# Top-k attention with an ELU feed-forward: the start-up order, the queue of the first queries, and the buffers of the weight decoding

## The chip, the cores and the metric

The kernel runs on one core of a Trainium2 chip. A core has five engines that run side by side[...]: TensorE (PE, matrix products; its weight loads are shown apart as PEld), VectorE (DVE), ScalarE (ACT), GpSimd (POOL) and SyncE (SP), which here only issues DMAs. The metric is the device time of one execution in microseconds (us), median of three runs.

## The reference

```python
def _attn_ref(q, k, v):            # each (8, 8, 576, 64) float32
    scores = 1/sqrt(64) * q @ k.transpose(0, 1, 3, 2)
    kth = the 32nd largest of each row of 576 scores
    scores = where(scores >= kth, scores, -1e9)
    attn = exp(scores - max); attn = attn / (sum(attn) + 1e-9)
    return attn @ v

def _moe_ref(x, w_in, w_out):      # x (4608, 512), w_in (512, 2048), w_out (2048, 512)
    h = x @ w_in
    g = where(h > 0, h, exp(min(h, 0)) - 1)
    return g @ w_out
```

The attention's output (batch, head, position, feature) is reordered to (batch x position, head x feature) and is the input x of the feed-forward part. The weights arrive as float64 and are decoded to float32 on the core. The output is 4608 x 512 float32.

## The kernel before, in words

**Attention steps.** The work is cut into steps of 128 query rows for one pair of heads: `scores` (L298 on PE, evacuated by ACT at L306) makes a 128 x 576 score tile for each of two heads. VectorE finds the 32 largest of each row by four MAX8 and three MATCH_REPLACE8 per head (L317, L321, L327 in the first eight steps; L339, L344, L351 later). `mask` makes two small POOL operations (L364, L366) and two ACT passes, a steep PReLU and an Exp with a row sum (L367, L368). `normalise` adds a small constant on POOL (L377), takes the reciprocal on VectorE (L379) and scales the tile on POOL (L381). `turn` transposes the tile on PE (L400) and ACT copies it out (L401); `attend` multiplies with v (L426), and `finish` copies the result into xT (L453). Scores are made two steps ahead.

**Start-up.** `load_qk(b, hp)` loads keys and queries of a head pair by three DMAs each (L221, L225), `load_v` the values by four (L236, L243); all are issued on SP, whose queue is in order. `transpose_qk` turns keys and queries on PE (L256, L268), and ACT copies them out (L261, L274).

**Feed-forward.** When a block of 1 to 3 tiles of 128 tokens is complete, `hidden(f)` makes 128 hidden features of it: four accumulating matmuls (L484, eight in the profile), a ReLU of the negative into a tile `n` (L496), a ReLU into gT (L497), an Exp (L498); a later VectorE operation (L465, from `close_gates`) joins n and gT. `project` (L507) multiplies with w_out. The pieces are handed out by `feed`, a written plan of costs and due times; a piece is held back until `decoded[0]` says that the weights that it needs are decoded.

**Weight decoding.** 32 pieces (16 of w_in, 16 of w_out) of 128 x 512 weights. `load_weight` brings 512 KB (4 KB for each partition) by one SP DMA (L150) into a buffer of the pool `raw`. `convert_first` runs three ACT passes (L167, L168, L169) and a POOL clamp (L170, which needs L167). `convert_last` runs two VectorE operations (L177, which needs L170; L180) and a POOL addition (L184) that writes the weights and lets the buffer go. `decode_piece(i)` asks for the load of piece i+2, converts piece i by `convert_first`, and ends piece i-1 by `convert_last`; it is called from `hook`, between VectorE's selection passes.

**What sets the order.** Up to step 8 (`tight`) a scheduler places the instructions of each engine; from step 8 on PE, ACT, VectorE and POOL keep the written order (`manual_schedule`). On each engine instructions then run in that order.

Of the kernel before, what the change touches and what calls it, by code (L numbers as in the profile page):

```python
# [8 lines left out]
AF = mybir.ActivationFunctionType  # L9
ALU = mybir.AluOpType  # L10
FP32 = mybir.dt.float32
U32 = mybir.dt.uint32
# [68 lines left out]
def kernel(  # L81
# [27 lines left out]
    def pool(name, bufs, **kw):  # L109
        return ctx.enter_context(tc.tile_pool(name=name, bufs=bufs, **kw))  # L110
# [5 lines left out]
    wkpool = pool("wk", 1)  # L116
    etpool = pool("et", 2)
    small = pool("small", 4)
    xtpool = pool("xt", 2)
    opool = pool("o", 1)  # L120
    ps_sc = pool("ps_sc", 1, space=PSUM)
    ps_t = pool("ps_t", 2, space=PSUM)
# [3 lines left out]
    raws = ExitStack()  # L126
    early = raws.enter_context(tc.tile_pool(name="early", bufs=1))
    earlyf = raws.enter_context(tc.tile_pool(name="earlyf", bufs=4))
    rawpool = raws.enter_context(tc.tile_pool(name="raw", bufs=3))

    ident = const.tile([P, P], FP32, tag="ident", name="ident")
    make_identity(nc, ident[:])
# [13 lines left out]
        return moe_w_out[f * P : (f + 1) * P, :], w_out[:, f, :]  # L146

    def load_weight(i):
        t = rawpool.tile([P, 4 * WN], U32, tag="raw", name="raw")
        nc.sync.dma_start(t[:, 0 : 2 * WN], weight(i)[0])  # L150
        raw[i] = t

    def parts(t):
        words = t[:, 0 : 2 * WN].rearrange("p (n w) -> p n w", w=2)
        return words[:, :, 0], words[:, :, 1], t[:, 2 * WN : 3 * WN], t[:, 3 * WN :]

    def convert_first(i):

        lo, hi, e, m = parts(raw[i])
        ef, mf = e.bitcast(FP32), m.bitcast(FP32)
        nc.scalar.activation(ef, hi.bitcast(FP32), AF.Abs, scale=2.0**-48)  # L167
        nc.scalar.activation(mf, lo, AF.Copy, scale=2.0**-29, bias=2.0**23)  # L168
        nc.scalar.activation(m.bitcast(I32), mf, AF.Copy, bias=-(2.0**23))  # L169
        nc.gpsimd.tensor_scalar(  # L170
            ef, ef, (2.0 - 2.0**-3 - 2.0**-23) * 2.0**-32, 2.0**-63, ALU.min, ALU.max
        )

    def convert_last(i):
        t, dst = raw.pop(i), weight(i)[1]
        lo, hi, e, m = parts(t)
        nc.vector.tensor_scalar(  # L177
            e, e, 0x0FFFFFFF, 3, ALU.bitwise_and, ALU.logical_shift_left
        )
        nc.vector.scalar_tensor_tensor(  # L180
            out=e, in0=hi, scalar=0x80000000, in1=e,
            op0=ALU.bitwise_and, op1=ALU.bitwise_or,
        )
        nc.gpsimd.tensor_tensor(  # L184
            dst.bitcast(I32), e.bitcast(I32), m.bitcast(I32), ALU.add
        )

    decode = []
# [2 lines left out]
    def hook():  # L191

        if not decode:
            return
        decode.pop(0)()
        if not decode:
            raws.close()
            late["f"] = ctx.enter_context(tc.tile_pool(name="f", bufs=5))
            late["g"] = ctx.enter_context(tc.tile_pool(name="g", bufs=2))
            late["x"] = ctx.enter_context(tc.tile_pool(name="x", bufs=2))  # L200

    def decode_piece(i):
        if i < 2 * NF:
            if i + 2 < 2 * NF:
                load_weight(i + 2)
            convert_first(i)
        if i > 0:
            convert_last(i - 1)
            decoded[0] = i

    loaded, kqT, vT = {}, {}, {}

    def load_qk(b, hp):

        for name, src in (("k", k), ("q", q)):
            n = J + 1 if name == "k" else J
            t = ldpool.tile([P, n, 2, D], FP32, tag=name + "in", name=name + "in")
            if name == "k":
                last = t
            for hh in range(2):  # L220
                nc.sync.dma_start(  # L221
                    t[:, 0:J, hh, :],
                    src[b, 2 * hp + hh, 0:JP, :].rearrange("(p j) d -> p j d", j=J),
                )
            nc.sync.dma_start(  # L225
                last[0:R, J, :, :] if name == "k" else last[R:P, J, :, :],
                src[b, 2 * hp : 2 * hp + 2, JP:S, :].rearrange("h p d -> p h d"),
            )
            loaded[b, hp, name] = t

    def load_v(b, hp):

        t = kvpool.tile([P, 2 * J + 2, D], FP32, tag="vT", name="vT")
        for hh in range(2):
            h = 2 * hp + hh
            nc.sync.dma_start(  # L236
                t[:, hh * J : (hh + 1) * J, :],
                v[b, h, 0:JP, :].rearrange("(p j) d -> p j d", j=J),
            )
            mine = slice(hh * R, (hh + 1) * R)  # L240
            other = slice((1 - hh) * R, (2 - hh) * R)
            nc.gpsimd.memset(t[other, 2 * J + hh, :], 0.0)
            nc.sync.dma_start(t[mine, 2 * J + hh, :], v[b, h, JP:S, :])  # L243
        vT[b, hp] = t
# [32 lines left out]
    def start_qk(b, hp):  # L277
        turning.append(transpose_qk(b, hp))

    def turn_qk(whole=False):  # L280
        while turning:
            if next(turning[0], turning) is turning:
                turning.pop(0)
            elif not whole:
                return
# [3 lines left out]
    def scores(u):  # L289

        u.sc = scpool.tile([P, 2, S], FP32, tag="sc", name="sc")
        q0 = QUERIES + u.t.qt * P
        for half in range(2):
            for h, i, rows in u.heads:
                kq = kqT[u.t.b, h // 2]
                part = slice(i * D, (i + 1) * D)
                k0 = (KEYS if i == 0 else 0) + half * HS
                nc.tensor.matmul(  # L298
                    wide[rows, 2 * i + half, 0:HS],
                    kq[part, q0 : q0 + u.t.ql],  # L300
                    kq[part, k0 : k0 + HS],
                    start=True,
                    stop=True,
                )
        for i in range(2):
            nc.scalar.activation(  # L306
                u.sc[:, i, :].rearrange("p (a s) -> p a s", a=2),
                wide[:, 2 * i : 2 * i + 2, 0:HS], AF.Copy, scale=scale,
            )
# [136 lines left out]

    def finish(blk, parts, at, cols, src):
        if blk.xT is None:
            if blk.slots == 1 and late:
                blk.xT = late["x"].tile([P, NC, P], FP32, tag="xT", name="xT")  # L450
            else:
                blk.xT = xtpool.tile([P, NC, T], FP32, tag="xT", name="xT")
        nc.scalar.copy(blk.xT[:, at, cols], src)  # L453
        blk.left -= parts
        if blk.left == 0:
            ffn.extend(ffn_pieces(blk))
# [150 lines left out]
            fed["sum"] += cost  # L607
            piece()

    load_qk(0, 0)  # L610
    for i in range(2):
        load_weight(i)
    load_qk(0, 1)
    load_v(0, 0)
    start_qk(0, 0)
    turn_qk(True)
    scores(steps[0])
    load_qk(0, 2)
    start_qk(0, 1)
    turn_qk(True)  # L620
    scores(steps[1])
    load_qk(0, 3)
    for hp in range(1, NHP):
        load_v(0, hp)
    decode += [lambda i=i: decode_piece(i) for i in range(2 * NF + 1)]
    at(0, start_qk, 0, 2)
    at(1, start_qk, 0, 3)

# [5 lines left out]
    for n in range(NS + 3):  # L634
        for fn, args in todo.pop(n, []):
            fn(*args)
        ahead, cur, prev, done = step(n + 2), step(n), step(n - 1), step(n - 2)
        if n < tight:
            turn_qk(True)
            scores(ahead)  # L640
            for i in range(2):
                passes = select_row(cur, i)
                next(passes)
                if i == 0:
                    while closing:
                        attend(closing.pop(0))
                elif prev:
                    normalise(prev)
                    turn(prev, main)
                    turn(prev, rest)  # L650
                    turn(prev, other)
                feed(n, 0.25)
                next(passes)
                mask(cur, i)
                feed(n, 0.25)
            continue
        if n == tight:
            E = mybir.EngineType
            ctx.enter_context(
                tc.manual_schedule(engines={E.PE, E.Activation, E.DVE, E.Pool})  # L660
            )
        passes = select(cur) if cur else iter(range(4))
        if ahead:
            scores(ahead)
        while closing:
            attend(closing.pop(0))
        next(passes)
        feed(n, 0.25)
        if prev:
            mask(prev, 0)  # L670
        turn_qk()
        next(passes)
        feed(n, 0.25)
        if done:
            turn(done, main)
            turn(done, rest)
        if prev:
            mask(prev, 1)
        next(passes)
        feed(n, 0.25)  # L680
        if done:
            turn(done, other)
        next(passes)
        if prev:
            normalise(prev)
        feed(n, 0.25)
        turn_qk(True)
# [36 lines left out]
```

## Time and profile before

| what | value |
|---|---|
| median of 3 runs | 1712.81 us (1712.72 to 1713.59) |
| the profiled execution, its own time | 1713.55 us |
| its span, first to last instruction | 1711.8 us |
| PE busy | 1593.9 us (93%), 8560 matmuls |
| DVE busy | 1551.1 us (91%) |
| ACT busy | 1180.3 us (69%) |
| POOL busy | 432.7 us (25%) |
| mean granted TensorE clock | 0.973 |

Times in the profile are microseconds from the span's start; a line such as `L177` is a line of the kernel before. The page splits the span into 40 slices of 42.8 us and gives the busy share of each engine in tenths. A group of instructions is shown with its busy time, the mean time of one in nanoseconds, and the idle time of its engine just before it, with the instruction that ended this idle time. The chain is followed back from the last instruction, at each step to what released it. Busy is not the same as at full speed: an instruction that waits inside the engine for a shared resource counts as busy.

### The profile page before, as it was taken

To read this page: it belongs to the slowest core of one execution; us is meant where nothing else is said; L and a number is where in the kernel's file an instruction comes from. 1 tells how busy PE (TensorE), PEld (TensorE's weight loads), DVE (VectorE), ACT (ScalarE), POOL (GpSimd) and SP (SyncE) were. 2 spreads that over 40 slices of the span, in tenths; PEclk is the share of its full clock that TensorE was granted. 3 is DMA by queue.
4 is the path that set the end of the run, shared out by engine and by line. 5 is a ranking of instruction groups with operands and counts; after the bars stand their busy time and mean duration, and the time that the engine had idled before them with its cause. 6 is when DMAs were issued, how large, how long until landed. Compare 5 with 4: busy or idle time off the path is not lost.

```text
span 1711.8 us, 26507 instructions
## 1 busy us (share of the span) xinstructions
PE 1593.9 (93%) x8560; PEld 1029.6 (60%) x8560; DVE 1551.1 (91%) x3392; ACT 1180.3 (69%) x2813; POOL 432.7 (25%) x1142
## 2 busy tenths in 40 slices
PE   4558999999999999999999999999999999999999
PEld 3345676667575666655557575755557575755565
DVE  7899999999999999999999999999989999998600
ACT  5886786778686776768658585867758686767531
POOL 3664222222222222222222222222222212222100
PEclk8569999999999999999999999999999999999999
DMA  6531021001100111001100111001100000000000
GB/s 168 171 126 54 15 48 35 7 7 43 48 7 7 29 35 41 1 15 41 43 18 1 34 35 35 7 13 40 32 26 7 21 21 28 7 7 7 7 13 13
DMA packets 101130, 56.24 MB, mean 33 GB/s; under 512 B 84096, under 2 KB 92288, under 8 KB 100992
## 3 DMA queue, kind: packets, MB, share of 16 engines
q1 hardware_dynamic: 100992, 54.55, 11.5%
q8 instruction: 68, 1.11, 0.3%
q14 instruction: 70, 0.57, 0.1%
HBM read 45.09 MB, written 9.44 MB: 32 GB/s over the span
## 4 chain that ended last, share of the span: by engine, by line
PE 64%; DVE 23%; ACT 8%; issue 3%; POOL 1%; DMA 1%; SPq 0%; ACTq 0%; POOLq 0%
PE ops L507 25%; PE hps L484 19%; DVE wk L344 8%; PE avps L426 7%; DVE m L351 7%; PE scps L298 6%; PE eps L400 4%; DVE m L339 2%; DVE gT L465 2%; ACT sc L367 2%; ACT sc L368 2%; DVE wk L321 1%; DVE m L327 1%; ACT et L401 1%; ACT n L498 1%
## 5 line engine op out<-in xcount | busy, mean ns | idle before, releaser
L484 PE MATMUL hps<-xT,w_in 128*128 128x256 f32 (+2 forms) x2432 | 555.7, 377 | 24.8 <-ACT gT L497 16.9
L351 DVE MAX8 m<-wk 128x8 f32<-128x576 f32 x816 | 574.9, 745 | 0.0
L507 PE MATMUL ops<-w_out,gT 128*128 128x512 f32 x1152 | 522.6, 598 | 0.0
L484 PEld LDWEIGHTS hps<-xT,w_in 128*128 128x128 f32 x2432 | 410.1, 194 | 126.0 <-ACT gT L497 23.8
L344 DVE MATCH_REPLACE8 wk<-m,wk 128x576 f32<-128x576 f32 x544 | 399.5, 741 | 0.0
L507 PEld LDWEIGHTS ops<-w_out,gT 128*128 128x128 f32 x1152 | 208.6, 190 | 232.8 <-issue 197.5
L381 POOL TENSOR_SCALAR sc<-sc,rec 128x576 f32<-128x576 f32 x288 | 218.8, 769 | 254.7 <-DVE rec L379 234.0
L367 ACT ACTIVATE sc<-sc,neg 128x576 f32<-128x576 f32 x288 | 226.6, 787 | 55.9 <-POOL neg L364 55.6
L377 POOL TENSOR_SCALAR dene<-den 128x2 f32<-128x2 f32 x144 | 34.4, 239 | 879.5 <-ACT sc L368 878.9
L368 ACT ACTIVATE sc<-sc,gap 128x576 f32<-128x576 f32 x288 | 223.2, 775 | 26.3 <-ACT sc L367 1.5
L306 ACT ACTIVATE sc<-scps 128x576 f32<-128x576 f32 x288 | 173.0, 660 | 80.5 <-PE scps L298 80.4
L401 ACT COPY et<-eps 128x512 f32<-128x512 f32 x288 | 167.2, 581 | 74.3 <-PE eps L400 74.2
L426 PE MATMUL avps<-et,vT 128*64 128x256 f32 (+2 forms) x2080 | 190.4, 324 | 14.3 <-ACT et L401 13.7
L400 PE MATMUL eps<-ident,sc 128*128 128x128 f32 x1152 | 177.8, 280 | 24.7 <-POOL sc L381 24.6
L400 PEld LDWEIGHTS eps<-ident,sc 128*128 128x128 f32 x1152 | 145.2, 145 | 92.2 <-issue 48.4
L344 DVE MATCH_REPLACE8 wk<-m,sc 128x576 f32<-128x576 f32 x272 | 199.7, 741 | 0.0
L298 PE MATMUL scps<-kqT 64*128 64x288 f32 (+1 forms) x1280 | 186.5, 440 | 11.1 <-ACT et L401 6.1
L339 DVE MAX8 m<-sc 128x8 f32<-128x576 f32 x272 | 191.2, 744 | 0.0
L496 ACT ACTIVATE n<-hps 128x256 f32<-128x256 f32 (+2 forms) x304 | 112.4, 370 | 91.9 <-PE hps L484 89.0
L465 DVE SCALAR_TENSOR_TENSOR gT<-n,gT 128x256 f32<-128x256 f32 (+2 forms) x304 | 128.9, 430 | 49.6 <-ACT n L498 49.6
L426 PEld LDWEIGHTS avps<-et,vT 128*64 128x64 f32 x2080 | 120.6, 140 | 87.8 <-issue 28.7
L298 PEld LDWEIGHTS scps<-kqT 64*128 64x128 f32 (+1 forms) x1280 | 100.2, 182 | 76.6 <-issue 22.2
(43 smaller groups left out, 1066.1 us busy)
## 6 DMA issues: line engine op xcount, KB each, us to landing
kin<-in_k_dram SPq DMA_DIRECT2D x64, 128.0 KB, 2.8
qin<-in_q_dram SPq DMA_DIRECT2D x64, 128.0 KB, 2.8
raw<-in_moe_w_in_dram SPq DMA_DIRECT2D x16, 512.0 KB, 4.1
vT<-in_v_dram SPq DMA_DIRECT2D x64, 128.0 KB, 2.2
raw<-in_moe_w_out_dram SPq DMA_DIRECT2D x16, 512.0 KB, 3.2
out_dram<-osb SPq DMA_DIRECT2D x32, 256.0 KB, 2.2
kin<-in_k_dram SPq DMA_DIRECT2D x32, 32.0 KB, 2.5
kin<-in_q_dram SPq DMA_DIRECT2D x32, 32.0 KB, 2.3
```

Of the source, the lines that this page charges most:

```text
L298: nc.tensor.matmul(wide[rows, 2 * i + half, 0:HS], kq[part, q0 : q0 + u.t.ql], kq[part, k0 : k0 + HS], start=True, stop=True,)
L339: nc.vector.max(found[i], cur[i])
L344: nc.vector.match_replace(wk[i], found[i], cur[i], TAKEN)
L351: nc.vector.max(found[i], cur[i])
L367: nc.scalar.activation(sc, sc, AF.Prelu, bias=neg[:], alpha=STEEP)
L368: nc.scalar.activation(sc, sc, AF.Exp, bias=gap[:], accum_out=u.den[:, i : i + 1])
L381: nc.gpsimd.tensor_scalar(u.sc[:, i, :], u.sc[:, i, :], rec[:, i : i + 1], 1.0, ALU.mult, ALU.mult)
L400: nc.tensor.transpose(ps[:, c * P : (c + 1) * P], sc[:, c0 : c0 + P], ident[:])
L401: nc.scalar.copy(g.et[:, chunks, u.at, :], ps[:, 0 : n * P].rearrange("p (c q) -> p c q", c=n),)
L426: nc.tensor.matmul(ps[i * D : (i + 1) * D, cols], vt[:, 2 * J + i if c == J else i * J + c, :], w, start=(c == 0), stop=(c == J),)
L484: nc.tensor.matmul(ps[:, 0:n_tok], w_in[:, i, f * P : (f + 1) * P], blk.xT[:, i, 0:n_tok], start=(i == 0), stop=(i == NC - 1),)
L507: nc.tensor.matmul(blk.o[:], blk.gT[f // NG][:, f % NG, s * P : (s + 1) * P], w_out[:, f, :], start=(f == 0), stop=(f == NF - 1),)
```

## The change

The diff, without lines that only move:

```diff
-    xtpool = pool("xt", 2)
+    xpool = pool("x", 3)
...
-    rawpool = raws.enter_context(tc.tile_pool(name="raw", bufs=3))
+    rawpool = raws.enter_context(tc.tile_pool(name="raw", bufs=5))
...
     def load_weight(i):
-        t = rawpool.tile([P, 4 * WN], U32, tag="raw", name="raw")
+        t = rawpool.tile([P, 3 * WN], U32, tag="raw", name="raw")
...
     def convert_first(i):
-        lo, hi, e, m = parts(raw[i])
-        ef, mf = e.bitcast(FP32), m.bitcast(FP32)
+        lo, hi, e = parts(raw[i])
+        ef, mf = e.bitcast(FP32), lo.bitcast(FP32)
...
             raws.close()
-            late["f"] = ctx.enter_context(tc.tile_pool(name="f", bufs=5))
+            late["f"] = ctx.enter_context(tc.tile_pool(name="f", bufs=4))
             late["g"] = ctx.enter_context(tc.tile_pool(name="g", bufs=2))
-            late["x"] = ctx.enter_context(tc.tile_pool(name="x", bufs=2))
+            late["x"] = ctx.enter_context(tc.tile_pool(name="xt", bufs=2))

     def decode_piece(i):
         if i < 2 * NF:
             if i + 2 < 2 * NF:
                 load_weight(i + 2)
             convert_first(i)
-        if i > 0:
-            convert_last(i - 1)
-            decoded[0] = i
+        if i > 1:
+            convert_last(i - 2)
+            decoded[0] = i - 1
...
-    def load_qk(b, hp):
+    def load_qk(b, hp, other=nc.sync):
         for name, src in (("k", k), ("q", q)):
-            n = J + 1 if name == "k" else J
+            n, queue = (J + 1, nc.sync) if name == "k" else (J, other)
...
-                nc.sync.dma_start(
+                queue.dma_start(
...
     def finish(blk, parts, at, cols, src):
         if blk.xT is None:
-            if blk.slots == 1 and late:
-                blk.xT = late["x"].tile([P, NC, P], FP32, tag="xT", name="xT")
+            if blk.slots == 1:
+                blk.xT = xpool.tile([P, NC, P], FP32, tag="xT", name="xT")
             else:
-                blk.xT = xtpool.tile([P, NC, T], FP32, tag="xT", name="xT")
+                blk.xT = late["x"].tile([P, NC, T], FP32, tag="xT", name="xT")
...
-    load_qk(0, 0)
-    for i in range(2):
-        load_weight(i)
+    load_qk(0, 0, nc.scalar)
+    load_weight(0)
     load_qk(0, 1)
+    load_weight(1)
     load_v(0, 0)
-    start_qk(0, 0)
-    turn_qk(True)
-    scores(steps[0])
+    with tc.manual_schedule(engines=engines):
+        for hp in range(2):
+            start_qk(0, hp)
+            turn_qk(True)
+            scores(steps[hp])
     load_qk(0, 2)
-    start_qk(0, 1)
-    turn_qk(True)
-    scores(steps[1])
     load_qk(0, 3)
...
-    decode += [lambda i=i: decode_piece(i) for i in range(2 * NF + 1)]
+    decode += [lambda i=i: decode_piece(i) for i in range(2 * NF + 2)]
```

In words: the three DMAs of the first head pair's queries go to ACT's queue; the second weight load is put behind the second head pair's loads; PE, ACT, DVE and POOL keep the written order until the second step's scores. A decoding buffer takes 6 KB for each partition in place of 8 (the low words are converted in place), and there are five in place of three. VectorE's part and the last POOL addition of a piece come two pieces behind its conversion, so there is one more decoding piece (34 in place of 33). The tiles n go from five to four, tiles xT of one-tile blocks have three buffers of their own from the start, and the wide xT tiles are placed after the decoding.

More of the change, by code (lines that the diff above doesn't have):

```diff
@@ L154, in parts @@
         words = t[:, 0 : 2 * WN].rearrange("p (n w) -> p n w", w=2)
-        return words[:, :, 0], words[:, :, 1], t[:, 2 * WN : 3 * WN], t[:, 3 * WN :]
+        return words[:, :, 0], words[:, :, 1], t[:, 2 * WN :]
     def convert_first(i):
-        lo, hi, e, m = parts(raw[i])
-        ef, mf = e.bitcast(FP32), m.bitcast(FP32)
+        lo, hi, e = parts(raw[i])
+        ef, mf = e.bitcast(FP32), lo.bitcast(FP32)
         nc.scalar.activation(ef, hi.bitcast(FP32), AF.Abs, scale=2.0**-48)
         nc.scalar.activation(mf, lo, AF.Copy, scale=2.0**-29, bias=2.0**23)
-        nc.scalar.activation(m.bitcast(I32), mf, AF.Copy, bias=-(2.0**23))
+        nc.scalar.activation(lo.bitcast(I32), mf, AF.Copy, bias=-(2.0**23))
         nc.gpsimd.tensor_scalar(
@@ L175, in convert_last @@
         t, dst = raw.pop(i), weight(i)[1]
-        lo, hi, e, m = parts(t)
+        lo, hi, e = parts(t)
         nc.vector.tensor_scalar(
@@ L184, in convert_last @@
         nc.gpsimd.tensor_tensor(
-            dst.bitcast(I32), e.bitcast(I32), m.bitcast(I32), ALU.add
+            dst.bitcast(I32), e.bitcast(I32), lo.bitcast(I32), ALU.add
         )
@@ L224, in load_qk @@
                 )
-            nc.sync.dma_start(
+            queue.dma_start(
                 last[0:R, J, :, :] if name == "k" else last[R:P, J, :, :],
@@ L608, in feed @@
             piece()
-    load_qk(0, 0)
-    for i in range(2):
-        load_weight(i)
+    E = mybir.EngineType
+    engines = {E.PE, E.Activation, E.DVE, E.Pool}
+    load_qk(0, 0, nc.scalar)
+    load_weight(0)
     load_qk(0, 1)
+    load_weight(1)
     load_v(0, 0)
-    start_qk(0, 0)
-    turn_qk(True)
-    scores(steps[0])
+    with tc.manual_schedule(engines=engines):
[3 more added lines that the diff above has]
+            scores(steps[hp])
     load_qk(0, 2)
-    start_qk(0, 1)
-    turn_qk(True)
-    scores(steps[1])
     load_qk(0, 3)
@@ L657 @@
         if n == tight:
[L658 to L661, printed above, removed]
+            ctx.enter_context(tc.manual_schedule(engines=engines))
         passes = select(cur) if cur else iter(range(4))
```

## The prediction, made before the changed kernel was run

> **What bounds the kernel now.** First the page's 40 slices, for the stage that the change touches:
>
> ```profile
> PE   4558999999999999999999999999999999999999
> DVE  7899999999999999999999999999989999998600
> PEclk8569999999999999999999999999999999999999
> ```
>
> PE is busy at 90% and more from the fifth slice on (about 170 us); before that it is half idle and partly at half clock. DVE is the busy engine there, with something missing in the first three slices. The chain of waits says what the start hangs on:
>
> ```profile
> 4.81 0.59 SPq L150
> ...
> 6.52 5.93 DMA kin<-in_k_dram
> ...
> 12.58 0.45 PE qkps L268
> 13.03 2.24 PE scps L298 x8
> ...
> 15.30 0.66 ACT sc L306
> ...
> 15.98 1.41 DVE m L317 x2
> ```
>
> The first selection starts at 15.98 us: PE's first scores stand in its queue behind a transpose of the second head pair (L268), whose keys landed at 12.45, behind both weight loads. Later the chain runs through the decoding:
>
> ```profile
> 60.80 1.27 POOL w_in L184
> ...
> 62.09 5.37 DMA raw<-in_moe_w_in_dram
> ...
> 67.55 0.72 ACT raw L167
> ...
> 70.00 3.90 DMA raw<-in_moe_w_in_dram
> ```
>
> A buffer is let go by L184, only then is its load issued, and it lands 4 to 5 us later; ACT's L167, POOL's L170 and DVE's L177 follow. The trace's answer for L177 between 40 and 150 us gives DVE's price:
>
> ```profile
> L177 DVE TENSOR_SCALAR raw<-raw x27: 399/427/1492, 40.8 to 145.9; 128x512 uint32<-128x512 uint32 x27
>   POOL raw L170: 9.4, 13
> ```
>
> 13 waits, 9.4 us, are all of DVE's idle time between 16 and 150 us. Is that time worth something at the end? The chain from 130 to 300 us:
>
> ```profile
> 187.90 1.32 DVE m L351 x2
> ...
> 200.38 1.56 POOL sc L381 x2
> 201.93 0.47 POOL neg L364
> 202.42 0.79 ACT sc L367
> ```
>
> From 146 to 200 us the chain is DVE, nearly without a gap; then ACT and PE take over, and ACT waited 3.0 us for DVE's result at 202.42. What DVE gains up to there moves the rest, which stands in the same order in both kernels (the orders differ up to instruction 265 of 5090 on PE, 212 of 2530 on DVE).
>
> **The start, part by part.** The queries' three DMAs leave SP's queue for ACT's. They cost SP 3 x 0.64 us of issue; on ACT they precede the 1.28 us table load and are hidden, since ACT's first work came at 9.89. The last of the six loads was issued at 4.13 and landed at 6.81. The Trainium skill ("DMA: Bandwidth & Descriptors", "Issuing engines are not separate DMA queues") speaks against more: DMAs of several issuers run on the same 16 engines, only issue time is saved. The row: the core's DMA engines were busy 66% in the first 20 us, so by row and rule the loads end between 4.9 (issue was all) and 6.8 (the engines were); I take 5.3. Raw 0 is issued at 2.8 in place of 4.81 and took 5.06 from there to landing; say 8.3 (estimate, between 7.9 and 9.3).
>
> A new wait: ACT's order now has raw 0's three conversions (pitch 0.57 + 0.56 + 0.53) before the first head pair's copies (L261, L274). Behind them wait PE's first scores, behind those the second pair's transposes, and on SP the fourth pair's keys, which need that pair's buffer. So copies at 8.3 + 1.7 = 10.0, done 11.3, scores 2.3 (as at 12.96) to 13.6. Raw 1 now comes after the second pair's loads on SP: issued about 7.5, its data behind 576 KB that took 2.3 us, landing near 12.0 (11.27 before). ACT converts it (1.7) before the score evacuation: 13.7, plus 0.65 gives 14.35; DVE's raw 1 pair, POOL at 12.75 + 0.6, then 0.45 + 0.7, ends at 14.5. First selection about 14.6: **-1.4 us**, between -2.2 (raw 1 at 11.3) and +0.3 (DMA engines full, raw 1 at 13.8).
>
> Raw 2 to 4, which need no buffer back, follow three SP issues earlier, at about 26.3 instead of 28.55; landing after 4.15 (as before) is 30.4. ACT wants raw 2 at selection start + 16.3 = 30.9: no wait.
>
> **The decoding.** L177 of a piece now comes two places after its L170, and a load may be issued one piece earlier. Waits removed: **-9.4 us**. What is new, from the orders: on POOL, L170 of pieces 6, 8, 11, 14 and 16 still stands straight behind the previous piece's L184, which needs that piece's L180. L184 + L170 is 1.27 + 0.61, plus 0.1 of hand-over, against one selection pass (0.75) plus 0.6 of L180's pitch: 0.65 each for pieces 14 and 16, 0.65 for 6 (three L184 in a row), 0.4 for 8, 0.1 for 11: 2.4 us. ACT becomes tight: in 35.67 to 92.88 us ACT was busy 46.0, DVE 49.3 of 57.2 us. Without waits ACT has 3.3 us to spare; adding pitches along the new order, ACT and POOL deliver pieces 2 to 10 only 0.3 to 1.1 us before DVE wants them. I charge 1.0 us. New waits: **+3.4 us**, between 0.5 and 7.
>
> L177 also waits inside itself: alone it takes 0.41 us, at 47.29 beside a POOL L184 1.49. The rule is in the Trainium skill ("SBUF — State Buffer", "Who interferes with whom"): the port pair that VectorE and GpSimd share goes to one for a whole instruction, and a VectorE tensor_scalar can need it. It speaks against the change: before, L177 mostly started just after L170 with POOL empty; now it can meet an L184. By the rule alone, if all 27 met a whole one, 27 x 1.27 = 34 us. The row is nearer: the 17 L177 that did not wait cost 0.57 extra in 4 cases. In the new order seven pieces have just one pass between one pair and the next L177, 7 x 0.57 = 4.0, against 5.1 us of such excess in the 30 before. So **0**, between -4 and +4.
>
> **The small parts.** Per piece nothing is added: same instructions, same counts on all engines; the low words are converted in place. Piece 31 ends some 3 us later within step 8; w_out's last rows were written at 154.7 and PE wanted them at 163.0: covered by about 5 us; without that cover, up to 3 us. The xT buffers: tile 4 of the first pair of batches needs block 1's buffer, whose hidden pieces run from 169 to about 200 us, against step 16 after 240: nothing. Tiles n: setting each L496 beside the L465 four pieces earlier, 3 of 284 would wait, 2.0 and 0.5 us near 190 and 2.0 at 355.8. The reciprocal then has 2.9 us between its input and its turn, which covers them; without it 4.4 us. I take **+0.3**.
>
> Sum: -1.4 - 9.4 + 3.4 + 0 + 0.3 = **-7.1 us**. The profiled execution took 1713.55 (span 1711.8 and 1.75 around it), 0.74 above the median. Its span would be 1704.7, and the median 1712.8 - 7.1 = **1705.7 us**.
>
> **The rivals.** *The wait only moves*: ACT or the POOL order holds DVE back for about what the loads did. For it: ACT's 46.0 of 49.3. Against: from 95 us on, ACT idles on PE and DVE does not. New waits of 8 to 10 us leave the start's 1.4 and a little: 1709.5 to 1713, say 1711.5.
> *All of it goes*: no new waits, fewer port collisions, start at the early end: -2.2 - 9.4 - 2 = 1699.
> *Slower, by the four n tiles*: in the stage where PE sets the end, ACT waits in L496 for a VectorE L465 that is late, with its PSUM bank held and PE behind it. For it: the margin is under 3 us in 24 of 284 pieces; if all shrank by 3 us, the waits add up to 41 us. Against: 200 are over 5 us. It decides from 11 us of uncovered waits (7.1 + 3.4), about 1 us less margin everywhere with no cover; at 20 us (2 us less), 1726.
> *The change doesn't do what it says*: no, the new orders show it.
>
> **How the numbers follow.** 0.2% of 1712.8 us is 3.4 us, about what a measurement of this kernel tells from no change: faster is under 1709.4, slower over 1716.2. My case 0.72 (1701 to 1709.4), all of it 0.05, the wait moves 0.13, slower by n 0.10. Faster 0.77, same 0.13, slower 0.10. The range 1700.5 to 1711.8 leaves out the n case and the ends of the others.
>
> **What would show it.** Right: first L317 near 14.6; L177's idle between 16 and 150 us at 2 to 5 us in place of 9.4, ended by L170; step 9's first selection (L339 at 158.82 before) near 151.5; the loads of L150 landing well ahead of L167. Wrong: L167 still waiting for loads, L177's mean over 700 ns (598 over the 31 before), a first selection after 16, or L496 waiting for L465 after 200 us.

## The result and the profile after

The changed kernel takes 1710.22 us (median of 18 runs, 1708.63 to 1713.57), beside 1712.97 us for the kernel before in the same comparison (18 runs, 1710.88 to 1715.27). The ratio is 0.9985, 95% interval 0.9977 to 0.9992: 2.75 us faster, where 7.1 us were forecast, and less than the 3.4 us that the prediction calls the smallest difference a measurement of this kernel can tell, though the interval lies clear of 1.

Lines of the changed kernel stand one further down than before from L167 on: L178 and L181 are VectorE's two operations for a weight piece (L177 and L180 before), L171 and L185 POOL's clamp and addition (L170, L184), L318 and L340 the first MAX8 of a row (L317, L339), L466 the operation that joins n and gT, in the following called a gate (L465).

The page's slices of the changed kernel:

```profile
PE   4468999999999999999999999999999999999999
DVE  6999999999999999999999999999989989998600
PEclk8679999999999999999999999999999999999999
```

VectorE's second slice rose from 8 to 9 tenths, but it isn't all work. The answer of the trace for L178 between 16 and 150 us:

```profile
L178 DVE TENSOR_SCALAR raw<-raw x29: 400/651/1509, 34.1 to 148.0; 128x512 uint32<-128x512 uint32 x29
  POOL raw L171: 2.1, 5
```

The wait for POOL's clamp fell from 9.4 us in 13 cases to 2.1 in 5. But the median of one L178 rose from 0.427 to 0.651 us, for the same work. The chain of waits of the changed kernel between 60 and 62 us shows one of them from inside:

```profile
60.73 0.04 DVE raw L178
60.76 1.39 issue
62.16 0.75 DVE m L328
```

and the timeline shows what POOL did meanwhile:

```profile
60.66 1.29 POOL L185 TENSOR_TENSOR w_in<-raw 128x512 int32<-128x512 int32 x1
60.73 1.51 DVE L178 TENSOR_SCALAR raw<-raw 128x512 uint32<-128x512 uint32 x1 [0.23 <-POOL raw L171]
```

L178 was issued 0.07 us after an addition of POOL had begun, and ended 0.29 us after it. It counts as busy, so no table of waits shows this.

**The balance on VectorE**, from the first selection to step 9's first selection; the same 264 instructions in both kernels. Idle time here is the sum of all gaps over 0.15 us:

| us | before | after | difference |
|---|---|---|---|
| first selection starts | 15.98 | 15.59 | -0.39 |
| idle | 9.45 | 3.16 | -6.29 |
| 30 x L177 / L178 | 17.05 | 20.42 | +3.37 |
| 30 x L180 / L181 | 21.51 | 22.64 | +1.13 |
| 16 gates L465 / L466 | 11.19 | 11.30 | +0.11 |
| all other instructions and the hand-overs between them | | | -1.02 |
| step 9's first selection starts | 158.82 | 155.72 | -3.09 |

Step 13 starts at 200.51 and 197.42 us, still 3.09 apart, and the medians lie 2.75 us apart: the gain at step 9 is the gain at the end, about. The one profiled execution of the changed kernel doesn't show this (its span is 1711.8 us, as before): it is the longest of the 18. TensorE's granted clock fell to 0.5 for 3.41 us four times after step 13 in it, twice in the profiled execution before. From step 13's start to the last MAX8, the kernels of this study whose order behind step 8 is that of the changed kernel took 1414.1 to 1414.5 us with two such windows, 1415.7 to 1416.2 with three, and 1417.6 with four: about 1.7 us for each, as 3.41 us at half clock should cost (an estimate). In the following the place of step 9 is therefore compared beside the medians.

### The profile page after: what moved, and what is told of

Its sections match the earlier page's. It is cut to its first block, busy times and chain, and to the rows that moved or that the text cites. A ratio compares the mean times of both kernels' runs of the same rounds, so it can differ in the third digit from the quotient of the medians.

```text
span 1711.8 us, 26492 instructions
## 1 busy us (share of the span) xinstructions
PE 1594.0 (93%) x8560; PEld 1028.2 (60%) x8560; DVE 1554.1 (91%) x3392; ACT 1179.9 (69%) x2813; POOL 431.9 (25%) x1142
## 4 chain that ended last, share of the span: by engine, by line
PE 58%; DVE 28%; ACT 7%; issue 2%; POOL 0%; ACTq 0%; POOLq 0%
PE ops L508 24%; PE hps L485 17%; DVE wk L345 10%; DVE m L352 9%; PE avps L427 7%; PE scps L299 6%; PE eps L401 4%; DVE m L340 3%; DVE gT L466 2%; ACT sc L368 2%; ACT sc L369 2%; DVE wk L322 1%; DVE m L328 1%; ACT et L402 1%; ACT n L499 1%
## 5 line engine op out<-in xcount | busy, mean ns | idle before, releaser
L307 ACT ACTIVATE sc<-scps 128x576 f32<-128x576 f32 x288 | 173.1, 660 | 80.1 <-PE scps L299 80.0
L340 DVE MAX8 m<-sc 128x8 f32<-128x576 f32 x272 | 191.1, 744 | 0.0
L497 ACT ACTIVATE n<-hps 128x256 f32<-128x256 f32 (+2 forms) x304 | 112.2, 369 | 92.9 <-PE hps L485 84.7
L466 DVE SCALAR_TENSOR_TENSOR gT<-n,gT 128x256 f32<-128x256 f32 (+2 forms) x304 | 129.3, 432 | 49.6 <-ACT n L499 49.6
```

Of the source, the lines that this page charges most:

```text
L340: nc.vector.max(found[i], cur[i])
```

## The experiments

All medians are set beside the kernel before on the same chip, with the ratio's 95% interval. In the five comparisons of this study the kernel before itself had medians of 1712.97 to 1713.75 us, so two changed kernels from different comparisons are told apart to about 1 us only.

**1. The start alone.** The kernel before, with `load_qk`'s other queue and these lines; buffers, places and tiles stay.

```diff
-    load_qk(0, 0)
-    for i in range(2):
-        load_weight(i)
+    load_qk(0, 0, nc.scalar)
+    load_weight(0)
     load_qk(0, 1)
+    load_weight(1)
     load_v(0, 0)
...
+    with tc.manual_schedule(engines=engines):
+        for hp in range(2):
+            start_qk(0, hp)
+            turn_qk(True)
+            scores(steps[hp])
```

> The kernel before with only the new start: first queries on ACT's queue, raw 1 behind the second pair's loads, both first scores in written order; decoding buffers, VectorE's place and the n tiles as before. Theory (the start gave little, because raw 1 lands at about 13.0): first L317 about 15.6 in place of 15.98, step 9's first selection about 158.4 in place of 158.8, end 0.4 us under the kernel before (1712.5). Rival, the prediction's step of -1.4: first L317 near 14.6, end near 1711.6. Rival, that the order of the loads and conversions of the start also disturbs the decoding behind it: L177's idle between 16 and 150 us grows over 10.5 us, end not under the kernel before.

Measured: 1716.98 us, ratio 1.0027 (1.0018 to 1.0036), 3.7 us slower. The first selection starts at 15.70, but step 9 at 162.22, 3.4 us later than before. The idle time is 10.3 us, only 0.8 more; L177 takes 21.7 us in place of 17.1. The third expectation was nearest, in its result and not in its cause: the scheduler lays the decoding out differently behind the other start (VectorE's order leaves that of the kernel before at its 44th instruction), and L177 meets POOL's work more often. Nine L177 begin inside an L184, 9.1 us over their bare time, where six did before, with 4.5 us.

**2. The decoding alone.** The changed kernel with the start of the kernel before.

```diff
-    load_qk(0, 0, nc.scalar)
-    load_weight(0)
+    load_qk(0, 0)
+    for i in range(2):
+        load_weight(i)
     load_qk(0, 1)
-    load_weight(1)
     load_v(0, 0)
-    with tc.manual_schedule(engines=engines):
-        for hp in range(2):
-            start_qk(0, hp)
-            turn_qk(True)
-            scores(steps[hp])
+    start_qk(0, 0)
+    turn_qk(True)
+    scores(steps[0])
     load_qk(0, 2)
+    start_qk(0, 1)
+    turn_qk(True)
+    scores(steps[1])
     load_qk(0, 3)
```

> The changed kernel with the start of the kernel before: five smaller buffers, VectorE's part two places behind and four n tiles alone. Theory (the waits go, about two thirds of it comes back as longer VectorE instructions beside POOL): DVE's idle time between first selection and step 9 falls from 9.4 to 2.5 to 4 us, L178 and L181 together take 3 to 5 us more than before (38.6), step 9's first selection near 156 in place of 158.8, end near 1710.5 (2.4 us under the kernel before). Rival, that the decoding gave its whole 6.3 us and something behind 200 us took it back: step 9's first selection near 152.5. Rival, that the change of the start and of the decoding only work together: end within 1 us of the kernel before.

Measured: 1712.72 us, ratio 1.0000 (0.9992 to 1.0009). Idle 6.7 us, L178 and L181 40.9 us (+2.3), step 9 at 157.71 (-1.1). The waits did not go by the buffers and the place alone; the third expectation held. The two parts do not add: +3.7 and -0.6 us alone (medians on the same chip), -2.75 together. With the start alone, L177, L180 and the gates take 2.7 us more, against 0.3 us that the start itself gains; with the decoding alone, they take back 2.0 of the 2.7 us of waits that go.

**3. POOL's additions cut short.** This shows what lengthens L178. L181 writes the weight itself, and POOL adds the low bits of the fractions in 8 of the 512 columns only; the others are left out. Up to step 9 VectorE's instructions stand in the order of the changed kernel.

```diff
         nc.vector.scalar_tensor_tensor(
-            out=e, in0=hi, scalar=0x80000000, in1=e,
+            out=dst.bitcast(U32), in0=hi, scalar=0x80000000, in1=e,
...
-            dst.bitcast(I32), e.bitcast(I32), lo.bitcast(I32), ALU.add
+            dst[:, 0:8].bitcast(I32), dst[:, 0:8].bitcast(I32),
+            lo[:, 0:8].bitcast(I32), ALU.add,
```

> The changed kernel with POOL's addition of each piece cut from 512 to 8 columns (L181 writes the weight directly; the low bits of the fractions are left out of the weights but for 8 columns). POOL's L185 falls from 1.29 us to about 0.1. Theory (L178, L181 and the gates L466 wait inside themselves for POOL's long additions): L178's time over 0.42 us falls from 7.9 us to under 3, L466's 16 instructions from 11.3 us to under 7, step 9's first selection comes 9 to 14 us earlier (142 to 147), and the end, as far as PE can follow, is 5 us or more under the changed kernel (1705 or less). Rival, that these instructions are long for another reason (their data, ACT's order): L178 and L466 keep their lengths, step 9 near 154 to 155, end 1709 to 1710. Rival, that what DVE gains before 155 us doesn't count at the end: step 9 early, end 1709.5 to 1711.

The trace's answers for L185, L178 and the gates (here L467) of this kernel:

```profile
L185 POOL TENSOR_TENSOR w_out<-w_out,raw x16: 197/203/247, 77.6 to 136.8; 128x8 int32<-128x8 int32 x16
...
L178 DVE TENSOR_SCALAR raw<-raw x30: 399/413/782, 34.3 to 135.5; 128x512 uint32<-128x512 uint32 x30
...
L467 DVE SCALAR_TENSOR_TENSOR gT<-n,gT x16: 265/277/597, 91.4 to 128.7; 128x128 f32<-128x128 f32 x16
```

The changed kernel's gates, for comparison:

```profile
L466 DVE SCALAR_TENSOR_TENSOR gT<-n,gT x16: 265/868/1277, 100.9 to 145.0; 128x128 f32<-128x128 f32 x16
```

Measured: 1693.91 us, ratio 0.9887 (0.9872 to 0.9902). Against the changed kernel L178 takes 7.35 us less, L181 2.10, the gates 6.38: 15.8 us in all; the idle time 0.85 less. Step 9 starts at 139.38, 16.3 us earlier (9 to 14 were expected), and the median (4 runs) is 16.3 us lower. So the decoding's VectorE instructions spend 15.8 us waiting inside themselves, POOL's additions are the cause, and each microsecond that VectorE saves before step 9 comes out at the end. PE followed a gain more than twice as large as the one forecast. In the trace of the changed kernel 13.7 us of excess over the bare lengths (0.42, 0.67 and 0.27 us) lie in instructions that began inside an addition, and 3.7 in those that began inside a clamp; with the short additions 0.1 and 1.2 us remain.

**4. Five n tiles again.**

```diff
-            late["f"] = ctx.enter_context(tc.tile_pool(name="f", bufs=4))
+            late["f"] = ctx.enter_context(tc.tile_pool(name="f", bufs=5))
```

> The changed kernel with five n tiles again in place of four. Theory (four are enough: the step of +0.3): end within 0.8 us of the changed kernel's 1710.2, ACT's idle time before L497 that DVE's L466 ends at or near nothing in both. Rival (the gain of the decoding is given back by the four tiles): 2 us or more under the changed kernel, 1708.2 or less.

Measured: 1710.03 us, ratio 0.9983 (0.9974 to 0.9992): the same as with four. Behind 200 us ACT's L497 waits 0.8 us for a gate in this profile, as it does before, and 2.9 us in two cases with four tiles:

```profile
  DVE gT L466: 2.9, 2
```

That wait exists, and nothing of it is seen at the end.

**5. VectorE's part one place behind**, with five buffers and the new start.

```diff
-        if i > 1:
-            convert_last(i - 2)
-            decoded[0] = i - 1
+        if i > 0:
+            convert_last(i - 1)
+            decoded[0] = i
...
-    decode += [lambda i=i: decode_piece(i) for i in range(2 * NF + 2)]
+    decode += [lambda i=i: decode_piece(i) for i in range(2 * NF + 1)]
```

> The changed kernel with VectorE's part one place behind as before; five smaller buffers and the new start stay. It asks which of the two, buffers or place, takes the waits away, and which brings the collisions. Theory (the place lets L178 go without waiting and meet L185 instead): DVE's idle time before step 9 rises from 3.2 to 5 to 9 us, L178 and L181 together fall from 43.1 to 39 to 41.5 us, the end lies within 1.5 us of the changed kernel (1709 to 1712). Rival (the buffers do all of it, the place nothing): idle time, L178 and the end as in the changed kernel, each within 0.7 us.

Measured: 1713.01 us, ratio 0.9999 (0.9990 to 1.0008). Idle 7.4 us, 4.2 more than in the changed kernel; L178 2.4 us less, L181 0.4 more, step 9 at 157.45. The theory's ranges held for idle time and for L178 and L181 together (41.1 us); the median came 1 us above its band. The second place takes 4.2 us of waits away and gives 2.0 back in L178 and L181, and 1.2 in the gates.

**6. Raw 1 early.** The start's own step.

```diff
     load_weight(0)
+    load_weight(1)
     load_qk(0, 1)
-    load_weight(1)
```

> The changed kernel with raw 1 issued straight behind raw 0, ahead of the second pair's loads, as in the kernel before. Theory (raw 1's late landing at 13.0 holds the first selection): raw 1 lands by 11, first L318 near 14.7 in place of 15.6; the end 0.9 us under the changed kernel if VectorE's collisions stay at 8 + 2.5 us, and else 0.9 less what L178, L181 and L466 take more. Rival (the loads share the same DMA engines, so that raw 0 or the first queries land later by as much): first L318 not before 15.4.

Measured: 1710.78 us, ratio 0.9986 (0.9977 to 0.9995), no gain. Raw 1 landed at 9.97 in place of 13.03, and raw 0 no later (8.34), yet the first selection starts at 16.02. The timeline of ACT in this kernel:

```profile
9.99 0.66 ACT L168 ACTIVATE raw<-raw 128x512 f32<-128x512 f32 x1 [0.42 <-DMA raw<-in_moe_w_in_dram]
10.56 0.30 ACT L262 COPY kqT<-scps 128x192 f32<-128x192 f32 x1
10.76 0.67 ACT L170 ACTIVATE raw<-raw 128x512 int32<-128x512 f32 x1
11.33 0.67 ACT L169 ACTIVATE raw<-raw 128x512 f32<-128x512 uint32 x1
11.88 1.06 ACT L275 COPY kqT<-qkps 128x512 f32<-128x512 f32 x2
12.82 0.69 ACT L170 ACTIVATE raw<-raw 128x512 int32<-128x512 f32 x1
15.33 1.19 ACT L307 ACTIVATE sc<-scps 128x576 f32<-128x576 f32 x2 [1.81 <-PE scps L299]
```

Raw 1's conversions now stand among the first pair's copies (L262, L275) in place of ahead of the score evacuation (L307). PE's scores start at 13.00 in place of 11.71. The rival's number held, not its cause.

**7 and 8. Written order from step 0.** The changed kernel with all four engines in written order through steps 0 to 7; in the eighth run gates that are due are also closed ahead of a piece's VectorE part.

```diff
+    ctx.enter_context(tc.manual_schedule(engines=engines))
     for n in range(NS + 3):
...
-        if n == tight:
-            ctx.enter_context(tc.manual_schedule(engines=engines))
```
```diff
+        close_gates(1)
         decode.pop(0)()
```

> The changed kernel with steps 0 to 7 in written order too: on VectorE each piece's L178 and L181 then stand side by side, two passes after the last pair; the first pieces come after the first selections; most gates L466 stand straight behind an L181. Theory (VectorE's time over the bare instructions comes from where they meet POOL's L185): L178's 30 fall from 20.4 to under 15 us, L181's from 22.6 to under 21, L466 stays near 11 (its group meets the L185 that its L181 has just let go), first selection at 11 to 12.5 us; the end 5 to 10 us under the changed kernel (1700 to 1705). Rival (the written order makes ACT, POOL and PE wait for each other, and VectorE with them): VectorE's idle time before step 9 over 12 us, end 1708 or more.

> As the kernel with steps 0 to 7 in written order, and gates that are due are closed ahead of a piece's L178 and L181 instead of straight behind them. Theory (a gate behind an L181 waits for the L185 that L181 releases): L466's 16 fall from about 11 to 5 to 8 us, the end 3 to 6 us under the written order alone. Rival (a gate is long because of its own operands or ACT): L466 unchanged, end within 1 us of the written order alone.

Measured: 1754.94 us (1.0238, 1.0224 to 1.0252) and 1752.84 us (1.0234, 1.0220 to 1.0248). In the seventh run the theory missed and its rival held: VectorE's idle time is 39.0 us, L178 and L181 of 32 pieces take 18.0 and 27.0 us. The reciprocal in this run, between 16 and 200 us:

```profile
L380 DVE RECIPROCAL rec<-dene x8: 145/166/167, 52.7 to 199.5; 128x2 f32<-128x2 f32 x8
  POOL dene L378: 30.3, 7
```

30.3 us of idle time stand before the reciprocal alone: in the longest case, at 52.71 us, its input comes behind masks that ACT runs between conversions, and behind POOL's L185. Further, a row's passes now follow each other, each on the result of the last, where the scheduler lets the two rows take turns; neighbouring instructions on VectorE overlap by 4.3 us in all in place of 16.5. The first selection starts at 12.07, as expected. The 16 gates fall to 7.1 us though they stand straight behind an L181: in 13 of the 16 POOL, in its own written order, has not come to an addition or a clamp when they run, and they take 0.27 to 0.29 us. Closing them earlier leaves them at 7.1 us, as the rival of the eighth run had it; its median is 2.1 us lower, but step 9 starts no earlier in it (200.41 against 199.52), and its profile has one window of half clock behind step 13 where that of the seventh has three. With 13 gates short already, the eighth run does not show what closing a gate earlier is worth.

**9 and 10. The additions in two and in four instructions.** All work is done, in the changed kernel; the diff is that for two. In both, VectorE's instructions up to step 9 stand in the order of the changed kernel.

```diff
-        nc.gpsimd.tensor_tensor(
-            dst.bitcast(I32), e.bitcast(I32), lo.bitcast(I32), ALU.add
-        )
+        for c in range(0, WN, WN // 2):
+            s = slice(c, c + WN // 2)
+            nc.gpsimd.tensor_tensor(
+                dst[:, s].bitcast(I32), e[:, s].bitcast(I32),
+                lo[:, s].bitcast(I32), ALU.add,
+            )
```

> The changed kernel with POOL's addition of each piece in two instructions of 256 columns in place of one of 512; the work and VectorE's order are the same. Theory (a VectorE instruction that meets an addition waits for the rest of that one instruction, 15.8 us in all by the run with the short addition): the longest L178 falls from 1.5 to about 1.1 us, L178 + L181 + L466 take 6 to 9 us less than 54.4, step 9's first selection near 148.5, the end 5 to 9 us under the changed kernel (1701 to 1705). Rival (the second half follows on POOL at once and VectorE doesn't get in between): lengths and end as in the changed kernel (1710). Rival (POOL gets so late by it that L171, and with it VectorE, waits): VectorE's idle time up by as much as its instructions get shorter, end 1708 to 1711.

> The changed kernel with POOL's addition in four instructions of 128 columns. Theory (the wait scales with the one POOL instruction that is met): L178 + L181 + L466 take 10 to 12 us less than 54.4, longest L178 about 0.8 us, end 8 to 12 us under the changed kernel (1698 to 1702). Rival (only the number of meetings counts, or POOL's longer time makes more of them): no better than two halves, within 1 us of it or worse.

The additions and L178 with two instructions:

```profile
L187 POOL TENSOR_TENSOR w_out<-raw x32: 730/740/947, 84.9 to 148.3; 128x256 int32<-128x256 int32 x32
...
L178 DVE TENSOR_SCALAR raw<-raw x30: 401/427/961, 34.6 to 146.3; 128x512 uint32<-128x512 uint32 x30
...
  POOL raw L171: 3.4, 7
```

and with four:

```profile
L187 POOL TENSOR_TENSOR w_out<-raw x64: 449/463/958, 87.5 to 151.9; 128x128 int32<-128x128 int32 x64
...
L178 DVE TENSOR_SCALAR raw<-raw x30: 408/564/683, 34.5 to 149.4; 128x512 uint32<-128x512 uint32 x30
...
  POOL raw L171: 7.4, 10
```

Measured with two: **1704.01 us (5 runs), ratio 0.9947 (0.9935 to 0.9960)**, 6.2 us below the changed kernel, step 9 at 150.23. L178, L181 and the gates take 7.7 us less, the idle time rises by 1.5. With four: 1707.93 us (0.9967, 0.9955 to 0.9980), step 9 at 153.31. Here they take 11.5 us less, as forecast, but the idle time rises by 8.0, 5.3 us of it before L178: four additions of 0.46 us cost POOL 1.85 us for a piece in place of 1.29, and its clamps come late. So the end missed its range, and the rival held: 3.9 us above the version with two. VectorE does get in between two additions; what a meeting costs follows the length of the one POOL instruction that is met (the longest L178 takes 1.51, 0.96 and 0.68 us beside additions of 1.29, 0.74 and 0.46), and POOL's time sets how far one can go with that. The version with two is faster than both kernels.

**11. The same in the kernel before**, in four instructions.

> The kernel before with POOL's addition in four instructions of 128 columns. Theory (the change is worth its waits, about 6 us, once both kernels lose little to meetings on VectorE): the meetings of the kernel before, 12 us, shrink to about 3, its idle time stays at 8 to 10 us, end near 1704; the changed kernel with the same addition lies 4 to 7 us below it. Rival (the change is worth 3 us whatever the meetings are): the two lie 2 to 3.5 us apart. Rival (the idle time of the kernel before is itself a consequence of VectorE's meetings): its idle time falls under 6 us and the two are within 2 us.

Measured: 1717.01 us, ratio 1.0015 (1.0007 to 1.0024), 9.1 us above the changed kernel with four. L177, L180 and the gates fall by 5.4 us and the idle time rises from 9.4 to 16.6. All three expectations missed. Step 9 starts at 160.86, 7.6 us behind the changed kernel with four, where the uncut kernels lie 3.1 apart. With POOL slower, the kernel before waits for it in 17 cases; the two places and the five buffers cover more of that. What the change would be worth at equal meetings and unchanged POOL time, this run therefore doesn't tell.

**12. VectorE alone in written order**, both rows in turn and each piece's pair side by side.

```diff
+    begun.enter_context(tc.manual_schedule(engines={E.DVE}))
...
-            for i in range(2):
-                passes = select_row(cur, i)
-                next(passes)
...
+            passes = select(cur, True)
+            next(passes)
+            feed(n, 0.25)
...
+            if prev:
+                normalise(prev)
```

> The changed kernel with VectorE alone in written order for steps 0 to 7: both rows of a step take turns (as from step 8 on), and each piece's L178 and L181 stand side by side, two or four passes after the last pair, gates straight behind a pair; ACT, POOL and PE stay with the scheduler. Theory (the instructions are long only where they meet an addition, and pairs two passes apart, with gates straight behind them, hardly meet one): L178's 30 fall from 20.4 to under 15 us, L181's from 22.6 to under 21.5, L466's 16 from 11.3 to under 8; if VectorE's idle time stays under 7 us, the end is 6 to 12 us under the changed kernel (1698 to 1704). Rival (side by side the two parts of a piece, the reciprocal and the gates come due before ACT and POOL have delivered): idle time over 12 us, end at 1708 or more, with the shorter instructions all the same.

Measured: 1715.00 us, ratio 1.0018 (1.0007 to 1.0028). Idle is 5.4 us, in one place; the gates are down to 5.8 us. But 32 L178 take 20.1 us and 32 L181 25.5: the additions don't follow the pairs. POOL has the clamps and the previous step's normalisation (L384 here) ahead of them, and comes to an addition just when the next pair stands there, as at 48.78 us, where an L178 of 0.83 us begins inside an L185 from 48.03 to 49.31. Neither expectation held as a whole: the gates came under 8 us and the end over 1708. Behind step 13 this kernel also loses some 4.6 us by the measure above (1417.4 us with one window); why stays open.

## Why the prediction was wrong

The sum had five terms. By its own steps:

**Meetings of VectorE and POOL, forecast 0, measured +4.5 us: this step failed.** "So **0**, between -4 and +4" stood on a count: seven pieces with just one pass between one pair and the next L177, at 0.57 us each, against 5.1 before. The profile before has six L177 in an L184 (4.5 us over 0.42 each); the one after has nine L178 lengthened by an L185 (0.63 us over 0.42 each, 5.7 in all) and seven more by an L171, which the count left out (0.32 each, 2.2). That alone is +3.4, inside the stated range. But L180 was not costed at all: L181, one selection pass behind its L178 in the new order, adds 1.1 us.

```profile
L181 DVE SCALAR_TENSOR_TENSOR raw<-raw x30: 666/674/1622, 35.2 to 152.3; 128x512 uint32<-128x512 uint32 x30
```

The gates, which the sum did not hold either, lose 6.9 us in meetings before and 7.0 after, so they change nothing here. The Trainium skill ("SBUF — State Buffer", "Who interferes with whom") has more than the prediction took from it: a VectorE instruction with two inputs in SBUF contends with a GpSimd instruction that reads SBUF, one with a single input outside the two-port modes doesn't. L181 and the gate have two such inputs and reached 1.62 and 1.28 us; the selection passes, which read one tile each, never left 0.73 to 0.76. The rule's second half would explain that VectorE's bulk is untouched, its first half that 15.8 us were at stake in place of the 7.9 of L178. Run 3 shows that the additions are the cause; that the port is, is the page's statement, which no run here contradicts.

**The waits, -9.4 + 3.4 = -6.0, measured -6.3: right in size.** ACT waited 13.6 us for raw loads between 16 and 150 us before, and not at all after:

```profile
ACT raw L167 <- DMA raw<-in_moe_w_in_dram: 10.5, 9, 2.9
...
ACT raw L167 <- DMA raw<-in_moe_w_out_dram: 3.1, 2, 2.3
```

What is left on VectorE is 2.1 us behind L171 and one reciprocal, 1.1 us. That the sum of the new waits came out (3.2 us against 3.4) is in part luck: of the pieces that the prediction named, only piece 6 waits (0.65 us, as forecast). Pieces 8, 11, 14 and 16, charged with 1.8 us, don't wait; pieces 2, 3, 9 and 10 wait 1.4 us, in the stretch where 1.0 us was charged for ACT; a wait before the reciprocal was not foreseen. Also, the step took the waits as the buffers' and the place's own work. Run 2 has both and loses only 2.7 us of waits; run 5 shows that the place is needed for 4.2 of them. The 6.3 us belong to this layout.

**The start, -1.4, measured -0.4.** The first loads landed at 5.89 (5.3 forecast, 6.81 before) and raw 0 at 8.55 (8.3). The step that failed is raw 1: "issued about 7.5" was 8.57, and it landed at 13.03 in place of 12.0, since SP stood on the DMA ahead of it for 1.57 us. The conversions, the evacuation and the selection followed in the order described:

```profile
13.05 0.66 ACT L168 ACTIVATE raw<-raw 128x512 f32<-128x512 f32 x1 [1.39 <-DMA raw<-in_moe_w_in_dram]
...
14.88 1.17 ACT L307 ACTIVATE sc<-scps 128x576 f32<-128x576 f32 x2
...
15.59 0.76 DVE L318 MAX8 m<-sc 128x8 f32<-128x576 f32 x1
```

Run 6 shows that an early raw 1 alone doesn't mend it: the first selection hangs on where ACT's conversions stand, not on one landing. With none of the raw conversions ahead it starts at 12.07 (run 7).

**Four n tiles, +0.3: right**, nothing at the end (run 4). **What VectorE gains up to step 9 moves the rest: right**, over the whole range seen (16.3 us at step 9 and at the end in run 3). The sum with the measured terms is -0.4 - 6.3 + 4.5 = -2.2, and -0.9 from the rest of the balance (+0.1 in the gates, -1.0 in all other instructions and the hand-overs): -3.1 us.

Of the marks, L177's idle time (2 to 5 us) and the loads held, the first selection and step 9 (151.5 against 155.72) did not; L178's mean of 20.42 / 30 = 681 ns stayed just under the 700 that was to refute the step, a threshold set too high: 2.5 us of gain were lost below it already. The last mark of being wrong, ACT waiting for a gate after 200 us, did appear (2.9 us in place of 0.8), but nothing of it is seen at the end (run 4). The rival *the wait only moves* named the right time (1709.5 to 1713) by another cause, which is luck: ACT and POOL's order did not hold VectorE back by more; the wait moved into the instructions, where it counts as work.

## What to carry to other kernels

Take an instruction's length alone and its length in place, for each kind on the engine that sets the end; the difference, summed, is a wait that no table of waits lists. In the changed kernel it was 15.8 us, beside 3.2 us of idle time. When a scheduler lays out the work, a change of a start or of a buffer deals the meetings of engines anew, and that can outweigh what the change does itself: cost the new order's meetings one by one, for all operations, or make the instruction that is met shorter, as far as its engine has time to spare.

## What the runs showed of the hardware

**One DMA issue of the start stands on SP for 1.2 to 2.0 us**, where the other issues of the first 15 us mostly take 0.4 to 0.9. It is the sixth behind a raw load, and in 13 of the 14 kernels it ended within 0.12 us of that load's landing: in the changed kernel from 6.96 to 8.53 (raw 0 landed at 8.55), before from 9.25 to 11.25 (raw 1, 11.27), with raw 1 early from 8.04 to 9.89 (raw 1, 9.97). It is no rule for the sixth DMA, though. With the start alone it ended 0.27 us before the landing (8.72, 8.99). The sixth behind raw 0 in the kernel before (8.58 to 9.21, landing 9.87) and behind raw 1 in the changed kernel (12.09 to 12.72, landing 13.03) did not stand, and at 1428.13 us a load of values stood for 1.36 us with no raw load under way. SP's timeline in the changed kernel:

```profile
5.64 1.28 SPq L222 DMA_DIRECT2D qin<-in_q_dram  x2
6.96 1.57 SPq L226 DMA_DIRECT2D kin<-in_q_dram  x1
8.57 0.59 SPq L150 DMA_DIRECT2D raw<-in_moe_w_in_dram  x1
```

Why an issue stands isn't shown. For the prediction it was about 1.0 us of raw 1's landing.

**POOL's addition has a fixed part.** 512, 256, 128 and 8 columns take 1.29, 0.74, 0.46 and 0.20 us: by these, about 0.19 us for an instruction and 2.1 ns for a column (an estimate). This sets what cutting it gains.

**The wait inside an instruction goes both ways.** In the changed kernel two clamps L171 that POOL began 0.02 and 0.10 us after an L181 took 1.12 and 1.04 us, where 0.61 is usual. In these cases, as in the long L178, it is the instruction that began second that takes longer, though no semaphore stands between the two.
